# Attention, Mish layer and experts in one kernel: beside attention only eight first products, held unactivated; Mish and every second product behind it

## The chip, the cores and the metric

One core of one Trainium2 chip runs the whole program in one launch. The metric is device time in microseconds: 1038.68 us, median of 3 runs (1038.64 to 1038.86).

## The reference

Three stages follow each other; inputs are float32, the weights of the second stage float64.

```
a      = near(q,k,v) + repeat4(far(mean4(q), mean4(k), mean4(v)))   # 2 batches, 8 heads, 576 positions, 64 wide
         # near: softmax over keys less than 4 away; far: softmax over all 144 means of 4
x      = a as [1152 tokens, 512]
h      = x @ w_in            # 512 -> 2048
x      = (h * tanh(log1p(exp(h)))) @ w_out         # Mish, 2048 -> 512
P      = exp(x @ w_gate), then 8 rounds of row and column normalization
out    = sum over 8 experts e of P[:, e] * (relu(x @ w1[e]) @ w2[e])
```

## The kernel before

**Stages.** (1) Attention, for 12 tiles of 96 tokens. A tile has a near part: scores on TensorE (PE), row maxima on VectorE (DVE), exponentials on ScalarE (ACT, `pl`), scaling on DVE, transposes on PE, their copy on ACT (`pt`), values on PE, then `join` on DVE, `xhi` on ACT and `xlo` on DVE (lines 852 to 872). The far part (`pg`) is alike, per half batch. `xhi` and `xlo` are the layer's input split in two, so that a float32 product is three matmuls: hi x hi, hi x lo, lo x hi. (2) The Mish layer. Its 2048 inner columns are 8 blocks `j` of 256, a block is two chunks of 128, and the tokens are three groups `g` of 384 (four tiles). A chunk has a first product (12 matmuls of 384 columns: `x @ w_in`), Mish, and a second product (12 matmuls onto four banks of PSUM). `SEGS` (line 31) lists in which order groups and blocks go; a chunk's second product stands `LAG` = 4 chunks behind its first. (3) The experts.

**Who sets the order.** Attention is ordered by a planner (`Plan`, line 146): every step has an engine and a cost in `COST` (line 38); `lay` lays the steps out many times with varied priorities, and the best of `PASSES` tries is emitted, each engine's order fixed by `pin` (line 579). Where PE would wait, it inserts small filler matmuls (`warm`, line 594). Beside attention the plan also takes 12 chunks (groups 0 and 1, blocks 0 to 2): 12 first products (`p_gemm1`, line 946), their Mish as nine steps, all from the exponentials' table (Exp, clamp, product, Ln, product, Exp, product, `ghi`, `glo`, lines 973 to 993), and 8 second products (`p_gemm2`, line 995). It also converts the first six weight pieces from float64 (`p_raw`, `p_split`) and four halves more.

Behind it stands the loop (line 1090, 28 steps): `w_raw` and `w_split` convert weights, then `gemm1(s)` and `gemm2(s - LAG)`. Here Mish is one ACT function (`mish`, line 504), from another table. The loop is ordered by the Tile scheduler; `tc.issue_after(last["pe"])` (line 1101) holds the instructions of its block on PE, and on PE only, behind the plan's last PE instruction. ACT's table loads are put in by the compiler wherever the next function needs another table.

The last eight chunks and the experts are laid out by a second planner run (`plan2`). It takes the PSUM banks from a ring (`RB2`, line 1120); its first matmuls are L1219 (`p_half1`).

Of the kernel before, what the change touches and what calls it, by code (L numbers as in the profile page):

```python
# [8 lines left out]
F32 = mybir.dt.float32  # L9
# [8 lines left out]
TQ = 96  # L18
# [12 lines left out]
SEGS = [(0, (0, 1, 2)), (1, (0, 1, 2)), (2, (0, 1, 2, 3, 4, 5)), (1, (3, 4, 5)), (0, (3, 4, 5)), (0, (6, 7)), (1, (6, 7)),  # L31
# [10 lines left out]
    "qk": ("ACT", 0.375, 0.5), "means": ("DVE", 0.67, 0.75), "small": ("DVE", 0.08, 0.14), "max": ("DVE", 0.5, 0.58), "fmax": ("DVE", 0.37, 0.45),  # L42
# [3 lines left out]
    "vsum": ("DVE", 0.34, 0.42), "vsum2": ("DVE", 0.6, 0.68), "e": ("ACT", 0.38, 0.53), "clamp": ("POOL", 0.64, 0.68), "m": ("DVE", 0.48, 0.56),  # L46
    "ln": ("ACT", 0.51, 0.62), "mh": ("DVE", 0.47, 0.55), "inv": ("ACT", 0.415, 0.53), "g": ("DVE", 0.475, 0.56),
    "ghi": ("ACT", 0.415, 0.55), "glo": ("POOL", 1.08, 1.13), "raw": ("ACT", 0.56, 0.68), "shift": ("DVE", 0.34, 0.45),
    "sign": ("DVE", 0.62, 0.71), "tail": ("DVE", 0.62, 0.71), "whi": ("ACT", 0.53, 0.68), "wlo": ("POOL", 1.25, 1.3),
    "sum": ("ACT", 0.375, 0.53), "load": ("SP", 0.45, 0.0),  # L50
# [22 lines left out]
PORT = {"shift", "sign", "tail", "m", "g", "scale", "fscale", "guard", "vsum", "vsum2", "clamp", "glo", "wlo", "wsum", "form", "formlo", "wl", "formlo2", "mult", "pairlo", "sums", "lows"}  # L73
# [14 lines left out]
EXTRA = 4  # L88
# [10 lines left out]
SEED, SEED2, NOISE, OTHER, SLACK = 11, 21, 0.1, 0.3, 5.0  # L99
# [228 lines left out]
def attn_moe_moe_kernel(  # L328
# [44 lines left out]
    def f32(a):  # L373
        return a.bitcast(F32)
# [9 lines left out]
    two = ap.tile([128, 48], F32, name="two", bufs=1)  # L384
# [14 lines left out]
    DVE.memset(two, 2.0)  # L399
# [18 lines left out]
    loads = []  # L418
    for i, (g, j, _, _) in enumerate(items):
        if i == 0 or j not in [x[1] for x in loads[-NBUF:]]:  # L420
            loads.append((i, j))
    last_of = {g: max(i for i, x in enumerate(items) if x[0] == g) for g in range(len(TPG))}
    ATT_END = 2 * next(i for i, x in enumerate(items) if x[0] == len(TPG) - 1)

    order = [j for _, j in loads]
    need = {(kind, m): 2 * loads[m][0] + LAG * (kind == 2) for m in range(len(order)) for kind in (1, 2)}
# [47 lines left out]
    def w_split():  # L474

        n = place["split"]
        place["split"] += 1
        kind, m = ring[n]
        hi, lo = (new(ap, [128, 1024], F32R, f"{z}{kind}", NBUF) for z in ("hi", "lo"))
        split(wraw.pop(n), hi, lo)  # L480
        whl[kind, order[m]] = hi, lo

    def ends():

        out = []
        for m, (i, j) in enumerate(loads):
            again = [x for x, y in loads[m + 1:] if y == j]
            out.append(max(x for x, y in enumerate(items) if y[1] == j and x < (again or [len(items)])[0]))
        return out

    def free_at(n):

        kind, m = ring[n]
        if m < NBUF:
            return 0
        return 2 * sorted(ends()[:m])[m - NBUF] + 2 + (LAG if kind == 2 else 0)
# [6 lines left out]
    gq, acc, ysum, gl = {}, {}, {}, {}  # L503
    def mish(hps, n):

        ghi, glo = (new(ap, [128, NMAX], F32R, z, LAG)[:, 0:n] for z in ("ghi", "glo"))
        ACT.activation(out=hps, in_=hps, func=AF.Mish)
        last["mish"] = ACT.activation(out=ghi, in_=hps, func=AF.Copy)
        DVE.tensor_tensor(out=glo, in0=hps, in1=f32(ghi), op=ALU.subtract)
        return ghi, glo  # L510

    def gemm1(s):
# [10 lines left out]
        gq[s] = mish(bk, n)  # L523
# [84 lines left out]
    def fixed(ts):  # L608
# [10 lines left out]
    mt = ap.tile([128, 6 * NMAX], F32, name="mt", bufs=1)  # L619
    RE, RMM, RL = (Ring(2, lambda i, o=o: mt[:, NMAX * (2 * o + i):NMAX * (2 * o + i + 1)]) for o in range(3))  # L620
    RGH, RGL = (tiles(ap, [128, NMAX], F32R, z, LAG) for z in ("ghi", "glo"))
    ys0, ys1 = new(yp, [128, 3 * NMAX], F32, "ysum", 1), new(ap, [128, NMAX], F32, "ysum1", 1)
    RYS = Ring(1, lambda i: [ys0[:, NMAX * d:NMAX * d + NMAX] for d in range(3)] + [ys1])

    RRAW = Ring(RAWB, raw_place)
    RHL = {kind: Ring(NBUF, lambda k, kind=kind: tuple(new(ap, [128, 1024], F32R, f"{z}{kind}", NBUF)
                                                       for z in ("hi", "lo"))) for kind in (1, 2)}
# [181 lines left out]
    def p_near(t):  # L809
# [60 lines left out]
        add("xhi", lambda: ACT.activation(out=hi_, in_=y(), func=AF.Copy), r=[("b", id(bk))], w=[("xhi", t)], b=[bk])  # L870
# [4 lines left out]
    late = 2 * NBUF  # L875
# [50 lines left out]
    def p_split(n):  # L926
        kind, m = ring[n]
        y = rawb[n]
        wbuf[kind, order[m]] = z = Buf(RHL[kind])

        def whi(c):
            whl[kind, order[m]] = z.t
            ACT.activation(out=z.t[0][:, c], in_=y.t[:, c], func=AF.Copy)
# [9 lines left out]
    gbuf, accb, ysb = {}, {}, {}  # L943
    piece = {(kind, order[m]): n for n, (kind, m) in enumerate(ring[:late])}

    def p_gemm1(s):
# [29 lines left out]
        def glo_():
            POOL.tensor_tensor(out=v_(go), in0=v_(e), in1=f32(v_(gh)), op=ALU.subtract)
            gq[s] = v_(gh), v_(go)

        add("e", lambda: ACT.activation(out=v_(e), in_=hps(), func=AF.Exp), r=[("h", s)], w=[("e", s)], b=[bk, e], rank=1)  # L980
        add("clamp", lambda: POOL.tensor_scalar(out=v_(e), in0=v_(e), scalar1=EXP20, scalar2=0.0, op0=ALU.min, op1=ALU.max),
            w=[("e", s)], b=[e], rank=1)
        add("m", lambda: DVE.scalar_tensor_tensor(out=v_(m), in0=v_(e), scalar=2.0, in1=v_(e), op0=ALU.add, op1=ALU.mult),
            r=[("e", s)], w=[("m", s)], b=[e, m], rank=1)
        add("ln", lambda: ACT.activation(out=v_(l), in_=v_(m), func=AF.Ln, bias=two[:, 0:1], scale=1.0), r=[("m", s)],
            w=[("l", s)], b=[m, l], rank=1)
        add("mh", lambda: DVE.tensor_tensor(out=v_(e), in0=v_(m), in1=hps(), op=ALU.mult), r=[("m", s), ("h", s)],
            w=[("e", s)], b=[bk, m, e], rank=1)
        add("inv", lambda: ACT.activation(out=v_(l), in_=v_(l), func=AF.Exp, scale=-1.0), w=[("l", s)], b=[l], rank=1)
        add("g", lambda: DVE.tensor_tensor(out=v_(e), in0=v_(e), in1=v_(l), op=ALU.mult), r=[("l", s)], w=[("e", s)],  # L990
            b=[e, l], rank=1)
        add("ghi", ghi_, r=[("e", s)], w=[("ghi", s)], b=[e, gh], rank=1)
        add("glo", glo_, r=[("e", s), ("ghi", s)], w=[("glo", s)], b=[e, gh, go], rank=1)

    def p_gemm2(s):
        g, j, h, first, end = chunks[s]
        n = groups[g][1] * TQ
        z, (gh, go) = wbuf[2, j], gbuf[s]
        if end:
            ysb[g] = Buf(RYS)  # L1000
        for d in range(KD):
            if first:
                accb[g, d] = Buf(RB, "acc")
                accb[g, d].kept = g == len(TPG) - 2
            bk = accb[g, d]
            o = slice(128 * d, 128 * d + 128)

            def pe(d=d, bk=bk, o=o):
                whi, wlo = (x.rearrange("p (a b) -> p a b", a=2) for x in z.t)
                acc[d] = bk.t  # L1010
                ghi, glo = gq[s]
                for i, (a, b) in enumerate(((whi, ghi), (whi, glo), (wlo, ghi))):
                    PE.matmul(out=bk.t[:, 0:n], lhsT=a[:, h, o], rhs=b, start=(first and i == 0), stop=(end and i == 2))
                if d == KD - 1:
                    gq.pop(s)
            add("gemm2", pe, r=[("ghi", s), ("glo", s)] + [(x, piece[2, j], i) for x in ("whi", "wlo") for i in range(2)],
                w=[("acc", g, d), "gemm2"], b=[bk, z, gh, go], rank=1)
            if end:

                def keep(d=d, bk=bk):  # L1020
                    ysum[g] = ysb[g].t
                    ACT.activation(out=ysum[g][d][:, 0:n], in_=bk.t[:, 0:n], func=AF.Copy)
                add("sum", keep, r=[("acc", g, d)], w=[("ys", g, d)], b=[bk, ysb[g]], rank=1)
# [56 lines left out]
    mine = [banks.index(accb[len(TPG) - 2, d].t) for d in range(KD)]  # L1080
# [9 lines left out]
    for s in range(ATT_END, S0):  # L1090
# [606 lines left out]
```

## Time and profile before

| | |
|---|---|
| median of 3 runs | 1038.68 us |
| profiled execution | 1039.66 us, of it 1037.7 us span |
| busy share of the span | PE 99%, DVE 68%, ACT 52%, POOL 40% |
| attention with its products | up to 136 us |
| loop of the Mish layer | 136 to 254 us |
| last chunks and experts | 254 to 1037.7 us |

The profile is of one execution. Busy is the time in which an engine had an instruction under way; matmuls overlap, so PE's cost is better read from the distance between starts.

### The profile page before, as it was taken

The page shows a single profiled execution, that of the slowest core. Times are in us where ns is not written, and L with a number is a line of the kernel's source. Part 1 is how long each engine was busy: PE and PEld are TensorE (multiplying, and loading weights), DVE is VectorE, ACT ScalarE, POOL GpSimd, SP SyncE. Part 2 cuts the span into 40 slices and gives each one's busy share as a digit, 9 for nine tenths or more (in the row PEclk, how much of TensorE's full clock was granted, in tenths as well). Part 3 has the DMA queues.
Part 4 walks back from the last instruction along what each step waited for, and adds up shares of the span by engine and source line. Part 5 has one row for each costly group of instructions (what it writes and reads, how often), then busy time and mean ns, then how long its engine had stood idle before and what let it go on. Part 6 is the DMA issues. An engine that isn't in the chain of part 4 may idle for free.

```text
span 1037.7 us, 17431 instructions
## 1 busy us (share of the span) xinstructions
PE 1027.7 (99%) x6421; PEld 933.0 (90%) x6421; DVE 709.4 (68%) x1359; ACT 535.5 (52%) x1378; POOL 413.8 (40%) x459
## 2 busy tenths in 40 slices
PE   8999999999999999999999999999999999999998
PEld 5888899999999988998999899989998899889997
DVE  6998854444578988876675766586666577657844
ACT  6888884434458434543545355534553455345531
POOL 0135232112236529553544254424552445345530
PEclk9999999999999999999999999999999999999999
DMA  9673212221004101210212012102120121111002
GB/s 217 169 169 92 78 61 83 85 78 42 1 11 132 54 8 62 62 56 5 62 61 62 1 62 62 62 1 61 62 62 7 55 61 62 25 37 61 22 1 92
DMA packets 47997, 63.41 MB, mean 61 GB/s; under 512 B 15272, under 2 KB 31656, under 8 KB 47912
## 3 DMA queue, kind: packets, MB, share of 16 engines
q1 hardware_dynamic: 47912, 62.30, 20.8%
q8 instruction: 50, 0.82, 0.3%
q14 instruction: 35, 0.29, 0.1%
HBM read 59.93 MB, written 2.36 MB: 60 GB/s over the span
## 4 chain that ended last, share of the span: by engine, by line
PE 73%; DVE 2%; ACT 1%; DMA 0%; issue 0%; DVEq 0%; ACTq 0%
PE bank L1612 38%; PE bank L1560 30%; PE bank L1237 2%; PE bank L1219 2%; PE bank L1392 1%; DMA raws<-in_moe_w_dram 0%; PE bank L1401 0%; DVE ysum L547 0%; DVE bank L1302 0%; ACT hhi L1377 0%; PE bank L1489 0%; DVE raws L464 0%; DVE hlo L1380 0%; ACT xs L1575 0%; ACT L1464 0%
## 5 line engine op out<-in xcount | busy, mean ns | idle before, releaser
L1575 ACT ACTIVATE xs<-bank 128x384 f32<-128x384 f32 x231 | 113.4, 492 | 262.2 <-PE bank L1560 240.8
L1612 PE MATMUL bank<-xs,hhi 128*128 128x512 f32 (+1 forms) x760 | 235.7, 391 | 0.0
L1628 DVE SCALAR_TENSOR_TENSOR yacc<-bank,P,yacc 128x512 f32<-128x512 f32 (+1 forms) x217 | 161.0, 747 | 93.6 <-PE bank L1612 92.0
L1612 PEld LDWEIGHTS bank<-xs,hhi 128*128 128x128 f32 x760 | 140.6, 188 | 19.7
L1535 POOL TENSOR_TENSOR wops<-wsums,wops 128x256 fp32r<-128x256 f32 x114 | 86.2, 767 | 160.9 <-ACT wops L1533 160.8
L1612 PE MATMUL bank<-xs,hlo 128*128 128x512 f32 (+1 forms) x380 | 148.8, 392 | 0.0
L1302 DVE TENSOR_TENSOR bank<-bank,xs 128x384 f32<-128x384 f32 x189 | 98.9, 560 | 46.4 <-ACT xs L1575 37.1
L1612 PE MATMUL bank<-wc,hhi 128*128 128x512 f32 x398 | 122.9, 390 | 0.0
L1560 PE MATMUL bank<-xform,wops 128*128 128x384 f32 x558 | 106.2, 335 | 0.0
L1560 PEld LDWEIGHTS bank<-xform,wops 128*128 128x128 f32 x558 | 98.0, 188 | 4.4
L1380 DVE SCALAR_TENSOR_TENSOR hlo<-bank,hhi 128x384 fp32r<-128x384 f32 x150 | 78.8, 550 | 16.3 <-ACT hhi L1377 13.8
L1612 PEld LDWEIGHTS bank<-wc,hhi 128*128 128x128 f32 x398 | 74.5, 188 | 15.5
L1377 ACT ACTIVATE hhi<-bank 128x384 fp32r<-128x384 f32 x150 | 70.4, 487 | 34.7 <-DVE bank L1302 29.8
L1302 DVE TENSOR_TENSOR wsums<-raws 128x256 f32<-128x256 f32 x147 | 63.5, 446 | 35.9 <-POOL wops L1535 17.9
L1612 PEld LDWEIGHTS bank<-xs,hlo 128*128 128x128 f32 x380 | 71.3, 188 | 16.2
L1612 PE MATMUL bank<-wc,hlo 128*128 128x512 f32 x199 | 78.2, 393 | 0.0
L1535 POOL TENSOR_TENSOR ysum<-wsums,ysum 128x256 fp32r<-128x256 f32 x59 | 45.0, 769 | 75.9 <-ACT ysum L1533 75.9
L1560 PE MATMUL bank<-xhi,wops 128*128 128x384 f32 x252 | 70.8, 337 | 0.3 <-ACT xs L1575 0.3
L1533 ACT ACTIVATE wops<-wsums 128x256 fp32r<-128x256 f32 x114 | 45.5, 413 | 33.6 <-PE bank L1560 28.6
L1422 POOL TENSOR_TENSOR xs<-temp,xs 128x512 fp32r<-128x512 f32 x42 | 58.4, 1412 | 9.9 <-ACT xs L1420 9.9
L472 POOL TENSOR_TENSOR lo<-raws,hi 128x512 fp32r<-128x512 f32 x20 | 26.5, 1338 | 75.2 <-ACT hi L471 69.4
L1560 PE MATMUL bank<-xform,ysum 128*128 128x384 f32 x282 | 54.8, 335 | 0.0
(241 smaller groups left out, 2255.5 us busy)
## 6 DMA issues: line engine op xcount, KB each, us to landing
temp<-in_moe_w_dram SPq DMA_DIRECT2D x64, 256.0 KB
raws<-in_moe_w_dram SPq DMA_DIRECT2D x16, 768.0 KB
raw<-in_moe_w_in_dram SPq DMA_DIRECT2D x16, 512.0 KB
raw<-in_moe_w_out_dram SPq DMA_DIRECT2D x16, 512.0 KB
raws<-in_moe_w_dram SPq DMA_DIRECT2D x5, 512.0 KB
rawq<-in_q_dram SPq DMA_DIRECT2D x4, 576.0 KB
rawv<-in_v_dram SPq DMA_DIRECT2D x8, 288.0 KB
vw<-in_v_dram SPq DMA_DIRECT2D x12, 192.0 KB
```

The costliest lines, as they stand in the source:

```text
L472: POOL.tensor_tensor(out=lo[:, c], in0=raw[:, c], in1=f32(hi[:, c]), op=ALU.subtract)
L1219: PE.matmul(out=bk.t[:, 0:NMAX], lhsT=a[:, kk, o], rhs=b[:, kk, c0:c0 + NMAX], start=(i == 0), stop=(i == 11))
L1302: eng.tensor_tensor(out=out, in0=a, in1=b, op=ALU.add if cb > 0 else ALU.subtract)
L1377: ACT.activation(out=hb.t[0], in_=bk.t[:, 0:TH], func=AF.Relu)
L1380: DVE.scalar_tensor_tensor(out=hb.t[1], in0=bk.t[:, 0:TH], scalar=0.0, in1=f32(hb.t[0]), op0=ALU.max, op1=ALU.subtract)
L1422: add("wlo", lambda raw=raw, y=y: POOL.tensor_tensor(out=y.t[:, 1], in0=raw(), in1=f32(y.t[:, 0]), op=ALU.subtract), r=[("r2", c), ("ch", ...
L1533: add("wh", lambda src=src, y=y: ACT.activation(out=y.t[:, 0], in_=piece(src), func=AF.Copy), r=key + rk, w=[("wh", r, n)] + wk, b=[y] + bs)
L1535: add("wl", lambda src=src, y=y: POOL.tensor_tensor(out=y.t[:, 1], in0=piece(src), in1=f32(y.t[:, 0]), op=ALU.subtract), r=key + [("wh", r ...
L1560: PE.matmul(out=bb.t[:, 0:TH], lhsT=y.t[:, wz, kk, :], rhs=x[xz][:, kk, :], start=(fresh and i == 0), stop=(i == 3 * KH - 1), skip_group_c ...
L1575: add("keep", lambda src=src, y=y: ACT.activation(out=y.t, in_=src.t[:, 0:TH], func=AF.Copy), r=[key, "late"], w=[("b", id(y))], b=[src, y])
L1612: PE.matmul(out=bk.t[:, a:b], lhsT=h[hz][:, js], rhs=y[:, wz, a:b], start=(f == fs[0] and i == 0), stop=(f == fs[-1] and i == 2))
L1628: DVE.scalar_tensor_tensor(out=y, in0=bk.t[:, a:b], scalar=p, in1=y, op0=ALU.mult, op1=ALU.add)
```

## The change

- `SEGS` starts with group 2 and goes on with 1 and 0 (before: 0, 1, 2). Only the four pairs (group, block) in `HELD`, eight chunks of groups 0 and 1, get their first product beside attention. Its result is copied to SBUF as it is, by ACT and DVE in turn (`holdA`, `holdD`), into the eight `ghi` and `glo` buffers that the loop uses later.
- The nine Mish steps, all second products and the partial sums (`ysum`) leave the plan. Attention may take six banks of PSUM at a time (before four).
- The plan converts three weight pieces and four halves (`LATE` = 3) instead of six and four.
- The loop has all 40 steps: for a held chunk only Mish, for the others first product and Mish; `gemm2(s - LAG)` from the fourth step on. Until the held chunks are through, `ghi` and `glo` lie in `xform`.
- `plan2` takes its banks in the order in which the loop has left them. Some buffers move, and the planner's seed is another.

```diff
+HELD = [(0, 0), (0, 1), (1, 0), (1, 1)]
-SEGS = [(0, (0, 1, 2)), (1, (0, 1, 2)), (2, (0, 1, 2, 3, 4, 5)), (1, (3, 4, 5)), (0, (3, 4, 5)), (0, (6, 7)), (1, (6, 7)),
+SEGS = [(2, (0, 1, 2)), (1, (0, 1, 2)), (0, (0, 1, 2, 3, 4, 5)), (1, (3, 4, 5)), (2, (3, 4, 5)), (0, (6, 7)), (1, (6, 7)),
...
-MOST = {"start": 8, "waves": 4, "gemm1": 1, "acc": 4}
+MOST = {"start": 8, "waves": 6, "gemm1": 2}
...
-    def mish(hps, n):
-
-        ghi, glo = (new(ap, [128, NMAX], F32R, z, LAG)[:, 0:n] for z in ("ghi", "glo"))
+    def mish(s, hps):
+
+        if s < SWITCH:
+            ghi, glo = (xform[:, s % (LAG + 1), z].rearrange("p a b -> p (a b)")[:, 0:NMAX] for z in range(2))
+        else:
+            ghi, glo = (new(ap, [128, NMAX], F32R, z, LAG) for z in ("ghi", "glo"))
         ACT.activation(out=hps, in_=hps, func=AF.Mish)
...
+    held_ = [new(ap, [128, NMAX], F32R, z, LAG) for z in ("ghi", "glo") for _ in range(LAG)]
...
-        add("e", lambda: ACT.activation(out=v_(e), in_=hps(), func=AF.Exp), r=[("h", s)], w=[("e", s)], b=[bk, e], rank=1)
...
+        def hold(i):
+            y = held[s] = f32(held_[i])
+            if i % 2:
+                DVE.tensor_copy(out=y, in_=bk.t[:, 0:n])
+            else:
+                ACT.activation(out=y, in_=bk.t[:, 0:n], func=AF.Copy)
+        i = len(held)
+        held[s] = None
+        add("holdD" if i % 2 else "holdA", partial(hold, i), r=[("h", s)], w=[("held", s)], b=[bk], rank=1)
...
-    for s in range(ATT_END):
+    for s in sorted((s for s, x in enumerate(chunks) if x[:2] in HELD), key=lambda s: chunks[s]):
         p_gemm1(s)
-        if s >= LAG:
-            p_gemm2(s - LAG)
...
-    for s in range(ATT_END, S0):
+    SWITCH = max(held) + 1
+    for s in range(S0):
...
         with tc.issue_after(last["pe"]):
-            gemm1(s)
-            gemm2(s - LAG)
+            if s in held:
+                mish(s, held.pop(s))
+            else:
+                gemm1(s)
+            if s >= LAG:
+                gemm2(s - LAG)
...
-    RB2 = Ring(8, lambda i: banks[i], MOST2)
+    w_, turn_ = of_tag["w"], turn["w"]
+    spots = w_[turn_ % 4 + 1:] + w_[:turn_ % 4] + [acc[d] for d in range(KD)] + [w_[turn_ % 4]]
+    RB2 = Ring(8, lambda i: spots[i], MOST2)
```

ACT's order in attention, in before, behind the last copies of kT (`pl`: near exponentials, `mt` and `ghi`: steps of Mish, `raws` and `hi`: weight conversion):

```order
L980 ACTIVATE mt<-bank_119 128x384
L905 ACTIVATE raws<-raw_1012 128x512
L974 ACTIVATE ghi<-mt 128x384
L870 ACTIVATE xhi<-bank_115 128x4x96
L985 ACTIVATE mt<-mt,two 128x384
L738 ACTIVATE pl_103,ld<-bank_120,lm 96x102
L989 ACTIVATE mt<-mt 128x384
L738 ACTIVATE pl_103,ld<-bank_120,lm 96x102
L905 ACTIVATE raws<-raw_1078 128x512
L738 ACTIVATE pl_103,ld<-bank_120,lm 96x102 x2
L980 ACTIVATE mt<-bank_116 128x384
L738 ACTIVATE pl_102,ld<-bank_117,lm 96x102 x3
```

and at the like place of the changed program, from the first hold on (L955; L495 is the Mish of the loop, here on a held chunk in `ghi`; L721 are the exponentials; L891 a weight half):

```order
L955 ACTIVATE ghi<-bank_118 128x384
L891 ACTIVATE raws<-raw_991 128x512
L495 ACT_TABLE_LOAD
L495 ACTIVATE ghi<-ghi 128x384
L721 ACT_TABLE_LOAD
L721 ACTIVATE pl_101,ld<-bank_115,lm 96x102 x4
L721 ACTIVATE pg_103,gd<-bank_111,gm 72x144 x2
L721 ACTIVATE pg_104,gd<-bank_117,gm 72x144 x2
L495 ACT_TABLE_LOAD
L495 ACTIVATE ghi<-ghi 128x384
L721 ACT_TABLE_LOAD
L721 ACTIVATE pg_106,gd<-bank_118,gm 72x144
```

The steps of Mish between the exponentials are gone; in their place stand Mish instructions of the loop, each between two table loads. The whole order has eight Mish of held chunks in front of attention's last `xhi` (L855) and, from this place to there, eleven table loads.

PE's order where the plan ends and the loop begins, in before (L957 planned first products, L540 second and L521 first products of the loop):

```order
L957 MATMUL bank_118<-xlo,hi_1088 128x384
L957 MATMUL bank_118<-xhi,lo_1089 128x384
L540 MATMUL bank_116<-ghi,hi_1352 128x384
L521 MATMUL bank_114<-xhi,hi_484 128x384
L540 MATMUL bank_116<-glo,hi_1352 128x384
L540 MATMUL bank_116<-ghi,lo_1353 128x384
```

and in the changed program (L838 the value products of the last attention tile, L942 planned first products, L509 first products of the loop):

```order
L942 MATMUL bank_117<-xhi,lo_646 128x384
L838 MATMUL bank_112<-pt,vw_96 64x96 x8
L509 MATMUL bank_113<-xhi,hi_471 128x384
L509 MATMUL bank_115<-xhi,hi_471 128x384
L509 MATMUL bank_116<-xhi,hi_645 128x384
L509 MATMUL bank_113<-xlo,hi_471 128x384
```

Before, the plan ends with first products of chunks whose tiles are long done; now it ends with a tile's values, and the loop's first products read that tile.

## Rows read from the trace of the kernel before

**Rows 1.** the page: busy time and share of the span; granted clock by slice

```profile
PE 1027.7 (99%) x6421; PEld 933.0 (90%) x6421; DVE 709.4 (68%) x1359; ACT 535.5 (52%) x1378; POOL 413.8 (40%) x459
...
PEclk9999999999999999999999999999999999999999
```

**Rows 2.** busy time in two stretches: us, then PE, PEld, DVE, ACT, POOL

```profile
14.00:136.00 122.00, 119.21 (x1599) 101.42 (x1596) 109.57 (x251) 105.92 (x404) 34.09 (x33) 1.00 0.54 132
300.00:1037.70 737.70, 734.05 (x3689) 660.49 (x3687) 517.31 (x978) 344.75 (x819) 335.04 (x385) 1.00 0.15 48
```

**Rows 3.** PE in order of time, the seam: start us, us, instruction

```profile
136.03 0.34 PE L540 MATMUL bank<-ghi,hi 128*128 128x384 f32 x1
```

**Rows 4.** line 540 on PE: durations ns, first to last start us

```profile
L540 PE MATMUL bank<-ghi,lo x112: 336/336/338, 136.5 to 252.3; 128*128 128x384 f32 x112
```

**Rows 5.** PE in order of time, behind the loop: idle before and its releaser

```profile
253.90 0.45 PE L1219 MATMUL bank<-xhi,hi 128*128 128x384 f32 x1 [1.23 <-DVE glo L509]
```

**Rows 6.** groups of instructions, 0 to 136 us: count, busy us, mean ns, idle

```profile
L985 ACT ACTIVATE mt<-mt,two 128x384 f32<-128x384 f32 x11 | 6.8, 619 | 2.0 <-DVE mt L983 2.0
L977 POOL TENSOR_TENSOR glo<-mt,ghi 128x384 fp32r<-128x384 f32 x10 | 11.2, 1117 | 20.0 <-issue 15.6 <-ACT ghi L974 4.4
```

**Rows 7.** PE in order of time, where both orders are cut

```profile
65.10 0.45 PE L957 MATMUL bank<-xhi,hi 128*128 128x384 f32 x1
```

**Rows 8.** PE in order of time, small matmuls between products

```profile
120.10 0.34 PE L957 MATMUL bank<-xlo,hi 128*128 128x384 f32 x1
120.36 0.67 PE L780 MATMUL bank<-ident,pg 72*72 72x72 f32 x8
...
121.14 0.42 PE L957 MATMUL bank<-xhi,lo 128*128 128x384 f32 x1
121.40 0.34 PE L957 MATMUL bank<-xhi,hi 128*128 128x384 f32 x1
```

**Rows 9.** groups of instructions, 0 to 136 us: the narrow fillers

```profile
L598 PE MATMUL bank<-identb 128*128 128x96 bf16 x47 | 3.0, 207 | 0.0
```

**Rows 10.** ACT in order of time, attention: a cost is the distance of starts

```profile
71.91 0.68 ACT L905 ACTIVATE raws<-raw 128x512 f32<-128x512 f32 x1
72.48 0.35 ACT L738 ACTIVATE pl<-bank,lm 96x102 f32<-96x102 f32 x1
...
72.80 0.35 ACT L738 ACTIVATE pl<-bank,lm 96x102 f32<-96x102 f32 x1
...
73.12 0.49 ACT L980 ACTIVATE mt<-bank 128x384 f32<-128x384 f32 x1
73.49 0.35 ACT L738 ACTIVATE pl<-bank,lm 96x102 f32<-96x102 f32 x1
...
74.45 0.65 ACT L933 ACTIVATE hi<-raws 128x512 fp32r<-128x512 f32 x1
74.97 0.36 ACT L738 ACTIVATE pl<-bank,lm 96x102 f32<-96x102 f32 x1
...
89.81 0.41 ACT L783 ACTIVATE pt<-bank 72x288 f32<-72x288 f32 x1
90.10 0.87 ACT L847 ACTIVATE pt<-bank 102x384 f32<-102x384 f32 x2
```

**Rows 11.** ACT in order of time, the seam: table loads and Mish

```profile
142.02 1.28 ACT L989 ACT_TABLE_LOAD   x1
143.32 0.52 ACT L989 ACTIVATE mt<-mt 128x384 f32<-128x384 f32 x1
...
147.54 0.47 ACT L507 ACTIVATE bank<-bank 128x384 f32<-128x384 f32 x1
148.05 0.49 ACT L508 ACTIVATE ghi<-bank 128x384 fp32r<-128x384 f32 x1
```

**Rows 12.** DVE in order of time: a tile's join and its xlo

```profile
130.18 0.57 DVE L861 TENSOR_TENSOR bank<-bank,odT 128x384 f32<-128x384 f32 x1 [0.28 <-PE bank L855]
...
131.58 0.55 DVE L871 TENSOR_TENSOR xlo<-bank,xhi 128x384 fp32r<-128x384 f32 x1
```

More of the change, by code (lines that the diff above doesn't have):

```diff
@@ L416, in attn_moe_moe_kernel @@
     NS = len(chunks)
[L418 to L421, printed above, removed]
     last_of = {g: max(i for i, x in enumerate(items) if x[0] == g) for g in range(len(TPG))}
-    ATT_END = 2 * next(i for i, x in enumerate(items) if x[0] == len(TPG) - 1)
-    order = [j for _, j in loads]
-    need = {(kind, m): 2 * loads[m][0] + LAG * (kind == 2) for m in range(len(order)) for kind in (1, 2)}
+    uses = {1: [(j, i) for i, (g, j, _, _) in enumerate(items) if (g, j) not in HELD], 2: [(x[1], i) for i, x in enumerate(items)]}
+    firsts = {(kind, j): min(i for x, i in u if x == j) for kind, u in uses.items() for j in range(NQ)}
+    lasts = {(kind, j): max(i for x, i in u if x == j) for kind, u in uses.items() for j in range(NQ)}
+    need = {z: 2 * i + (LAG if z[0] == 2 else 0) for z, i in firsts.items()}
     ring = sorted(need, key=need.get)
@@ L477, in w_split @@
         place["split"] += 1
-        kind, m = ring[n]
+        kind, j = ring[n]
         hi, lo = (new(ap, [128, 1024], F32R, f"{z}{kind}", NBUF) for z in ("hi", "lo"))
         split(wraw.pop(n), hi, lo)
[L481 to L489, printed above, removed]
+        whl[kind, j] = hi, lo
     def free_at(n):
-        kind, m = ring[n]
-        if m < NBUF:
+        kind, j = ring[n]
+        before = [x for k, x in ring[:n] if k == kind]
+        if len(before) < NBUF:
             return 0
-        return 2 * sorted(ends()[:m])[m - NBUF] + 2 + (LAG if kind == 2 else 0)
+        return 2 * lasts[kind, before[-NBUF]] + 2 + (LAG if kind == 2 else 0)
     for tag, n, dt in (("raw64", R64, U32), ("hi1", NBUF, F32R), ("lo1", NBUF, F32R), ("hi2", NBUF, F32R), ("lo2", NBUF, F32R)):
@@ L509, in mish @@
         DVE.tensor_tensor(out=glo, in0=hps, in1=f32(ghi), op=ALU.subtract)
-        return ghi, glo
+        gq[s] = ghi, glo
     def gemm1(s):
@@ L869, in p_near, with xhi_ @@
         add("join", join, r=[("od", b, half, i) for i in range(2)], w=[("b", id(bk))], b=[bk, od])
-        add("xhi", lambda: ACT.activation(out=hi_, in_=y(), func=AF.Copy), r=[("b", id(bk))], w=[("xhi", t)], b=[bk])
+        def xhi_():
+            last["mish"] = ACT.activation(out=hi_, in_=y(), func=AF.Copy)
+        add("xhi", xhi_, r=[("b", id(bk))], w=[("xhi", t)], b=[bk])
         add("xlo", lambda: DVE.tensor_tensor(out=lo_, in0=y(), in1=f32(hi_), op=ALU.subtract),
@@ L874, in attn_moe_moe_kernel @@
     r64, rawb = {}, {}
-    late = 2 * NBUF
+    late = LATE
     def p_load64(m):
@@ L941, in p_split @@
             add("wlo", partial(wlo, c), r=[("raw", 2 * n + i), ("whi", n, i)], w=[("wlo", n, i)], b=[y, z])
-    gbuf, accb, ysb = {}, {}, {}
-    piece = {(kind, order[m]): n for n, (kind, m) in enumerate(ring[:late])}
+    piece = {x: n for n, x in enumerate(ring[:late])}
     def p_gemm1(s):
@@ L987, in p_gemm1 @@
[L987 to L1023, printed above, removed]
@@ L1074, in attn_moe_moe_kernel @@
         p_half(i + 1)
[L1075 removed]
+    for s in sorted((s for s, x in enumerate(chunks) if x[:2] in HELD), key=lambda s: chunks[s]):
         p_gemm1(s)
[L1077 to L1078 removed]
     plan.run(PASSES, SEED, True)
[L1080 to L1081 removed]
+    over = [max((u.done for u in o.users), default=0.0) if o else 0.0 for o in RB.own]
+    free = sorted(range(8), key=lambda i: over[i])
+    of_tag.update(w=[banks[free[(i - 1) % 4]] for i in range(4)], acc=[banks[i] for i in free[4:]])
     place.update(load=2 * late + EXTRA + 2, raw=2 * late + EXTRA, split=late)
```

58 lines of the change are left out of this document (16 added, 42 removed), and 1 row of the table COST.

## The prediction

> **What bounds the kernel now.** I read the page first: TensorE is busy 99% of the span, at a granted clock of 0.9 or more in every slice, which is the 2.4 GHz level [rows 1]. A busy share of 99% says little about any one stage, so the stretches come next. In the attention stretch (14 to 136 us) three engines are nearly full together: PE 119.2, DVE 109.6 and ACT 105.9 of 122 us. Behind 300 us, the third stage, PE has 734.1 of 737.7 us and DVE and ACT about 70% and 47% [rows 2]. So the third stage is PE's alone, and attention is where an edit of ACT or DVE can count. Last I read PE in order of time at the seams. The last planned product starts one step before 136.03, where the loop's first matmul (L540) starts without a gap [rows 3]; the loop's last starts at 252.3 [rows 4]. The 28 pairs of products are 672 matmuls, so one costs (252.3 - 136.03) / 671 = 0.1733 us: the loop has no wait in it. At its end stands one, 1.23 us before L1219 at 253.90, for the `glo` of the last chunk [rows 5].
>
> So the sum has three terms: when the loop starts, how many matmuls it has, and the wait behind it. The third stage is left equal: on PE it has the same 2264 rows in the same 329 alternations of kind in both orders, though a few stand elsewhere around the gate.
>
> **What the loop gains.** Twelve chunks of first product and eight of second stood beside attention; now eight first ones do. Four first and eight second ones, 12 x 12 = 144 matmuls, move into the loop, which then has 816: 816 x 0.1733 = 141.4 us. ACT and DVE have room there: the eight held chunks need no first product, but by the order most of their Mish is already done, and the weights that move (three pieces) are converted one half per step as before. The wait behind the loop goes: before, the first bank taken is the one that the last chunk's Mish still reads; after, it is the one used three chunks earlier. I take the 1.23 us as gained, zero at worst.
>
> For break-even the loop must therefore start at 253.9 - 141.4 = 112.5 us, 23.5 us earlier than now.
>
> **What attention loses.** Each of the 12 chunks loses nine steps: on ACT four of 0.37 to 0.62 us, on DVE three of about 0.57, on POOL two, the dearer 1.12 [rows 6, 10, 12]. That frees 18 to 30 us of ACT and about 20 of DVE. Three pieces of weight less are six halves of 0.57 + 0.52 us on ACT [rows 10]. Four holds on ACT and four on DVE come in at 0.37 and about 0.57. All this lies beside PE and is worth only what PE waits for.
>
> To see what is left for PE I cut both orders at the same work. At 65.10 us in before PE has done 216 turn, 48 value and 64 near-score matmuls and 12 of first product (its next, L957, starts there) [rows 7]; in the changed order PE stands at exactly these counts behind its 12th matmul of first product, and with one filler less. Up to there nothing that PE waits for is removed (loads from HBM in the same order, the same conversions), so I take 65.1 us for both. Behind it, before takes 136.03 - 65.10 = 70.9 us: 228 matmuls of both products, 39.5 us; 31 blocks of them between small matmuls, each with two changes that make a start 0.26 us after the last instead of 0.17 [rows 8], 31 x 0.18 = 5.6; fillers 3.0 [rows 9]; so attention itself has 22.8. After keeps 22.8, has 84 matmuls, 14.6, in 18 blocks, 3.2, and two fillers: 40.6 us. By PE alone attention would end at 105.7.
>
> **What it adds, and the order shows this and not the diff.** A held chunk's Mish depends on nothing but its copy in SBUF, and the wrapper that keeps the loop's work behind the plan binds only PE. So all eight held Mish stand on ACT in front of the last `xhi` of attention, six of them in the middle of the softmax exponentials, which need another table. In front of that last `xhi` stand 11 ACT_TABLE_LOADs behind the cut, where before had none; before's four at the seam cost the loop nothing. One took 1.28 us, and the next activation started 1.30 us after it (142.02 to 143.32); a Mish of 128x384 took 0.51 to the next start [rows 11].
>
> The Trainium skill (ScalarE: Activation LUTs, "What ACT_TABLE_LOAD costs") gives the load the same 1283 ns, but adds about 1380 ns of drain to every switch. This trace shows the load and no such drain: the activation behind it starts 0.02 us after its end [rows 11]. By the page the 11 switches would cost 29.3 us, by the row 14.3.
>
> ACT's queue from the cut to the last `xhi`, counted in the changed order, at starts apart in [rows 10, 11]: 11 loads x 1.30 = 14.3; 8 Mish x 0.51 = 4.1; 48 exponentials x 0.32 = 15.4 (the 16 wider-row far ones priced as the near); 24 copies of 384 columns (transposed probabilities, `xhi`, qT, holds) x 0.37 = 8.9; 8 far ones x 0.29 = 2.3; 4 of odT at no more than that, 1.2; 4 halves of `hi` x 0.52 = 2.1; 2 raw halves x 0.57 = 1.1. Sum 49.4 us. Without loads, Mish and the four halves it is 28.9, which would have fitted under PE's 40.6 with 11.7 to spare. So ACT is late next: loads and Mish fill its spare time and 8.8 us more.
>
> Behind the cut comes the first hold and a raw half, so the 49.4 start at about 65.1 + 0.3 + 0.37 + 0.57 = 66.3 and end at 115.7. I walked ACT's rows against what PE and DVE must return: after most loads the operands are already there, since the engine comes late; a return trip of DVE, ACT, DVE takes 130.18 to 131.58 + 0.55, 1.95 us [rows 12], and the last load with its Mish covers the one behind the last exponentials. I put 1.0 us on the rest: 116.7. Then PE has nothing left: the plan now ends with the values of the last tile, directly followed by the first products of the third token group, which read that tile. Before had 30 matmuls to run there. Their first matmul needs `xhi`, the others `xlo`, 0.55 us later, partly covered by the first matmuls of two other chunks: 0.4. The loop so starts, in effect, at 117.1.
>
> **Sum.** 117.1 + 141.4 = 258.5 instead of 253.9: 4.6 us later. The profiled execution took 1039.66 us for a span of 1037.7, 0.98 over the median of the runs; the 4.6 is a difference inside the span, and I add it to the median: 1038.68 + 4.6 = 1043.3. Bounds: waits of ACT from 0 to 4, the hand-over 0 or 1.23, cut 65.1 give or take 1: 1041.5 to 1047.
>
> **Rivals.**
> - The loads run where ACT waits anyway, and PE stays the bound: end of attention 105.7, join, `xhi`, `xlo` 1.95, loop at 107.7, its end at 249.1: 4.8 us faster, 1033.9. For it: the scheduler put each Mish where it thought ACT idle, and a load issues without waiting for its operand. Against: the spare time is 11.7 us and the queue exceeds it by 8.8. It decides only if ACT enters the stretch 9 us ahead, which the first hold, waiting for PE, forbids.
> - About half of it: the softmax rows run early against PE's order, so that the loads cost 4 to 5 us less. The loop starts near 112.5, 1038 to 1040, no change. For it: three ring buffers more for attention in PSUM (six banks, not four).
> - The return trips are not overlapped: ACT's order was planned without the loads, and each of the six interruptions delays a tile by a whole trip, 6 x 1.95 = 11.7 instead of the 1.0: 1054. For it: ACT is in order, and [rows 2] shows DVE nearly as full as ACT. Against: DVE has lost about 20 us of work. A granted clock that falls when PE waits 2 to 3 us at a time, which no row here shows (the longest wait in them is the 1.23 of [rows 5]), would end in the same place.
> - Each switch costs more than its load: the engine runs empty before it and fills again behind it, at most two of the longest activations, 2 x 0.68 = 1.36 us a switch [rows 10]; 11 x 1.36 = 15.0, so 1058.3. For it: amid the exponentials the pipe is fuller than at the seam. Against: [rows 11]. The drain of the Trainium skill's page named above would be of this size.
>
> **Chances.** Forecast 0.64, faster rival 0.10, half way 0.10, return trips 0.13, emptying 0.03. The first lies wholly beyond 0.2% of the median (2.1 us, about what a measurement of this kernel can tell from no change), the half-way case wholly within: slower 0.80, same 0.10, faster 0.10. Range 1038.5 to 1050: it leaves out the faster rival and the far ends of the slow ones. The forecast's own range is 1041.5 to 1047.
>
> **What would show it.** Right: about ten table loads of 1.28 us on ACT between 65 and 117 us, ACT busy over 95% there, PE waiting some 9 to 11 us in that stretch for `pl`, `pt` or `xhi` of ACT; the loop's first L509 at 115.5 to 119; no gap within the loop, 0.173 us a matmul; no wait for `glo` in front of L1161. Wrong: the loop starting by 112 with ACT's loads in its idle time; a loop that waits for weights or for held chunks (the step of L495 and L496); or a clock below 1.00 behind 65 us.

## The result and the profile after

The changed kernel takes 1049.13 us (median of 4 executions, 1048.35 to 1053.03), the kernel before beside it 1038.66 (4 executions, 1038.22 to 1038.86): a ratio of 1.0109, 95% interval 1.0084 to 1.0134. It is slower by 10.5 us where 4.6 were forecast. The sign, the place and the mechanism came as forecast, the size did not: 1049.13 lies above the forecast's own range of 1041.5 to 1047 and only inside the wider one, 1038.5 to 1050, that left room for slow rivals. Each of the three terms of ACT's queue was a microsecond or more too small, and the clock did something that the forecast had left to a rival.

The page of the changed kernel, to be held against [rows 1]: TensorE's busy time is 1.2 us less, but the span is 9.2 us longer, and one slice of the granted clock, the fourth (79 to 105 us), is no longer at 9.

```profile
PE 1026.5 (98%) x6376; PEld 933.8 (89%) x6376; DVE 694.5 (66%) x1338; ACT 536.0 (51%) x1365; POOL 391.9 (37%) x435
...
PEclk9998999999999999999999999999999999999999
...
PE 90%; ACT 7%; DMA 2%; DVE 1%; issue 0%; DVEq 0%; ACTq 0%
```

The last line is from the chain that ended last: 7% of the span, some 70 us, run through ACT. So I looked at the two halves of attention behind the cut of [rows 7] (columns: stretch, length, then busy us of PE, PEld, DVE, ACT and POOL, granted clock, DMA share, GB/s).

```profile
65.00:95.00 30.00, 22.06 (x258) 17.65 (x260) 17.08 (x50) 28.89 (x86) 1.08 (x1) 0.90 0.16 35
95.00:125.00 30.00, 26.20 (x268) 22.92 (x265) 21.95 (x46) 25.43 (x82) 5.59 (x5) 0.99 0.28 82
```

In the first half ACT is busy 28.9 of 30 us while PE has 22.1: PE, full in [rows 2], now waits for ACT. The waits of PE between 65 and 136 us, by releaser (us in total, times, longest; before had two, 0.6 and 0.4):

```profile
PE bank L942 <- ACT pl L721: 2.4, 2, 1.9
PE bank L509 <- ACT xhi L855: 1.8, 1, 1.8
PE bank L803 <- ACT odT L788: 1.7, 1, 1.7
PE bank L828 <- ACT odT L788: 1.5, 1, 1.5
PE bank L838 <- ACT pt L830: 1.4, 1, 1.4
PE bank L763 <- ACT qT L667: 1.1, 1, 1.1
```

Together they and the smaller ones are 11.9 us, of which 11.3 end on ACT. ACT in order of time (start us, us, instruction, idle before and its releaser; the accumulator reads left out), first at the cut, then at the end of attention:

```profile
65.09 0.55 ACT L855 ACTIVATE xhi<-bank 128x384 fp32r<-128x384 f32 x1
65.46 0.56 ACT L955 ACTIVATE ghi<-bank 128x384 f32<-128x384 f32 x1
66.74 0.68 ACT L891 ACTIVATE raws<-raw 128x512 f32<-128x512 f32 x1 [0.72 <-DMA raw<-in_moe_w_out_dram]
67.44 1.28 ACT L495 ACT_TABLE_LOAD   x1
68.73 0.53 ACT L495 ACTIVATE ghi<-ghi 128x384 f32<-128x384 f32 x1
69.26 1.28 ACT L721 ACT_TABLE_LOAD   x1
70.56 0.34 ACT L721 ACTIVATE pl<-bank,lm 96x102 f32<-96x102 f32 x1
...
71.85 0.37 ACT L721 ACTIVATE pg<-bank,gm 72x144 f32<-72x144 f32 x1
72.21 0.38 ACT L721 ACTIVATE pg<-bank,gm 72x144 f32<-72x144 f32 x1
...
72.92 0.38 ACT L721 ACTIVATE pg<-bank,gm 72x144 f32<-72x144 f32 x1
73.41 1.28 ACT L495 ACT_TABLE_LOAD   x1
...
117.41 0.54 ACT L855 ACTIVATE xhi<-bank 128x384 fp32r<-128x384 f32 x1
119.17 0.63 ACT L463 ACTIVATE hi<-raws 128x512 fp32r<-128x512 f32 x1 [1.22 <-DVE raws L904]
119.71 0.51 ACT L495 ACTIVATE glo<-glo 128x384 f32<-128x384 f32 x1
120.12 0.48 ACT L855 ACTIVATE xhi<-bank 128x384 fp32r<-128x384 f32 x1
```

One held Mish (L495) amid the exponentials (L721) takes 67.44 to 70.56, 3.1 us, of which 2.6 are the two loads. Eleven loads stand between the cut and the last `xhi` (L855). On PE the 12th matmul of planned first products, behind which the prediction cut the order, starts at 63.73; the loop's first product follows the last `xhi`, and the third stage follows the loop's last product without the wait of [rows 5]:

```profile
63.73 0.33 PE L942 MATMUL bank<-xhi,lo 128*128 128x384 f32 x1
...
120.66 0.80 PE L509 MATMUL bank<-xhi,hi 128*128 128x384 f32 x3 [1.77 <-ACT xhi L855]
...
262.50 0.34 PE L528 MATMUL bank<-ghi,lo 128*128 128x384 f32 x1
262.67 0.34 PE L1161 MATMUL bank<-xhi,hi 128*128 128x384 f32 x1
```

### The profile page after: what moved, and what is told of

The parts are those of the page before. It is cut to its first block, busy times and chain, and to the rows that moved or that the text cites. A ratio compares the mean times of both kernels' runs of the same rounds, so it can differ in the third digit from the quotient of the medians.

```text
span 1046.9 us, 17277 instructions
## 1 busy us (share of the span) xinstructions
PE 1026.5 (98%) x6376; PEld 933.8 (89%) x6376; DVE 694.5 (66%) x1338; ACT 536.0 (51%) x1365; POOL 391.9 (37%) x435
## 4 chain that ended last, share of the span: by engine, by line
PE 90%; ACT 7%; DMA 2%; DVE 1%; issue 0%; DVEq 0%; ACTq 0%
PE bank L1554 38%; PE bank L1502 30%; PE bank L528 7%; PE bank L509 6%; PE bank L1179 2%; ACT pl L721 2%; PE bank L1161 2%; DMA raw<-in_moe_w_out_dram 1%; ACT pg L721 1%; ACT L495 1%; ACT L721 1%; PE bank L1334 1%; DMA rawq<-in_k_dram 0%; PE bank L654 0%; PE bank L1343 0%; PE bank L781 0%
## 5 line engine op out<-in xcount | busy, mean ns | idle before, releaser
L1554 PE MATMUL bank<-xs,hhi 128*128 128x512 f32 x760 | 235.7, 391 | 0.0
L1554 PE MATMUL bank<-xs,hlo 128*128 128x512 f32 x380 | 148.9, 392 | 0.0
L464 POOL TENSOR_TENSOR lo<-raws,hi 128x512 fp32r<-128x512 f32 x26 | 34.3, 1327 | 167.8 <-ACT hi L463 154.9
```

What stands on the lines that cost most here:

```text
L1554: PE.matmul(out=bk.t[:, a:b], lhsT=h[hz][:, js], rhs=y[:, wz, a:b], start=(f == fs[0] and i == 0), stop=(f == fs[-1] and i == 2))
```

## The experiments

The theory was that ACT's queue behind the cut, lengthened by loads and Mish, sets the start of the loop. Its rivals: the new order of attention is slow by itself; the return trips; the clock. In the changed kernel and its nine variants what lies behind the loop's first product (span less its start) is 926.2 to 927.8 us in the profiled execution, so that start is the number to read. Where two kernels have the same attention and differ only in a filled wait in front of the loop (the last three experiments), their starts lie 0.4 to 1.0 us apart: 107.36 and 106.33, 105.88 and 105.47, 120.66 and 121.22. No difference of that size is read as an effect. The kernel before, run beside each batch, had medians of 1038.65 to 1038.96. The start stands here with the loads and the Mish that ACT runs between the cut and the last `xhi`:

| kernel | loads | Mish | loop starts | median (executions) |
|---|---|---|---|---|
| changed | 11 | 8 | 120.66 | 1049.13 (1048.35 to 1053.03) |
| all held Mish behind | 0 | 0 | 105.88 | 1034.29 (1034.02 to 1035.77) |
| Exp for held Mish | 0 | 8 Exp | 107.36 | 1035.54 (1034.29 to 1037.05) |
| first four behind | 3 | 4 | 109.49 | 1038.35 (1036.77 to 1039.25) |
| last four behind | 8 | 4 | 117.64 | 1047.78 (1046.47 to 1048.51) |
| weight copies behind | 11 | 8 | 119.60 | 1048.65 (1047.99 to 1053.91) |

**All held Mish behind attention.** In the loop, and nothing else:

```
+    plan_end = last["mish"].ins          # the last xhi
 ...
             if s in held:
-                mish(s, held.pop(s))
+                with tc.issue_after(plan_end):
+                    mish(s, held.pop(s))
```

> The changed kernel, with one more order: the eight Mish steps of the held products (the Mish, its high part on ACT, the rest on DVE) may not be issued on ACT ahead of the last xhi of attention. Nothing else is changed. Theory (ACT's queue): in the changed kernel 11 table loads of 1.28 us and seven or eight Mish of 0.51 us, some 18 us, stand on ACT ahead of the last xhi at 120.1; without them ACT would be through at about 102, and TensorE's own work (40.6 us behind the first hold, so 105.7, with a microsecond or two of waits) sets the start of the loop at 107 to 109 instead of 120.7. The loop keeps its 142 us and the third stage its 784: 1035 to 1037. Rival (the new order of attention is slow by itself: no second products between attention's steps to fill TensorE, so it waits for transposes and copies as long as before): the loop starts at 117 or later, and the time stays above 1044. Rival (the Mish come due at the start of the loop and TensorE waits for them there): the loop is longer by 4 us or more, 1039 to 1042.

Measured: 1034.29 us, 0.9962 of before (0.9949 to 0.9974), so 14.8 less than the changed kernel and 4.5 less than before. ACT in this kernel, at the end of attention:

```profile
105.33 0.49 ACT L855 ACTIVATE xhi<-bank 128x384 fp32r<-128x384 f32 x1 [0.31 <-DVE bank L844]
105.72 0.67 ACT L453 ACTIVATE raws<-raw 128x512 f32<-128x512 f32 x1
106.41 1.28 ACT L495 ACT_TABLE_LOAD   x1
107.70 1.77 ACT L495 ACTIVATE glo<-glo 128x384 f32<-128x384 f32 x4
```

and PE there:

```profile
103.27 0.88 PE L838 MATMUL bank<-pt,vw 102*64 102x96 f32 x16
105.88 0.79 PE L509 MATMUL bank<-xhi,hi 128*128 128x384 f32 x3 [1.72 <-ACT xhi L855]
```

One load and the eight Mish now follow the last `xhi`. PE's own work in attention ends at 104.2, and the loop starts at 105.88, behind a wait of 1.72 us for that `xhi`. Both rivals fall: the new order of attention is faster than before's (the loop starts 6.6 us ahead of the break-even of 112.5), and the loop (to 247.86) takes 142.0 us, as in the changed kernel, without a wait for the late Mish.

**Exp in place of the held Mish.** The same instructions, no second table:

```
-        ACT.activation(out=hps, in_=hps, func=AF.Mish)
+        ACT.activation(out=hps, in_=hps, func=AF.Exp if s in exps else AF.Mish)   # exps: the held chunks
```

> The changed kernel, with Exp in place of Mish in the eight held chunks alone: the same instructions in the same order, but without a change of function table between attention's exponentials and the held chunks. It leaves Mish out of these chunks. Theory (table loads): ten or eleven loads of 1.28 us go, some 13 to 14 us of ACT's queue; the eight Exps of about 0.5 us stay. ACT is through at about 106 to 107, TensorE at 105.7 plus waits, so the loop starts at 107 to 110: 1036 to 1039. Rival (the return trips of the small products, not the loads, hold TensorE): 1045 to 1049. Rival (the loads cost only where TensorE is not waiting for something else, half of them): about 1042.

Measured: 1035.54 us, 0.9970 of before (0.9958 to 0.9981). The loop starts 13.3 us earlier than in the changed kernel, and 14.3 in the repeat of this attention with the filled wait (106.33). So of the 14.8 the loads are 13.3 to 14.3, 1.2 to 1.3 a load, and the Mish themselves the 0.5 to 1.5 that are left. This is what the loads were worth and not an upper bound of what one costs, because PE's own work, to 104.2, is the next limit. In its profile the clock fell behind the wait in front of the loop (columns as in the windows above):

```profile
104.00:107.00 3.00, 1.60 (x21) 1.16 (x19) 2.78 (x6) 1.78 (x5) 0.42 (x1) 1.00 0.06 16
107.00:110.00 3.00, 2.64 (x12) 2.50 (x13) 2.37 (x4) 1.05 (x3) 0.86 (x1) 0.82 0.50 164
110.00:113.00 3.00, 3.00 (x13) 3.00 (x12) 0.21 (x1) 2.70 (x4) 1.27 (x1) 0.62 0.62 173
```

PE is 1.60 busy of the 3 us before 107; behind that it runs 13 matmuls in 3 us instead of 19, and what follows the loop's start takes 927.8 us instead of 926.2.

**The bank order alone, in the kernel before.**

```
-    RB2 = Ring(8, lambda i: banks[i], MOST2)
+    RB2 = Ring(8, lambda i: spots[i], MOST2)     # spots as in the change
```

> The kernel before, with one part of the change alone: the order in which the third stage's plan is given the eight PSUM banks (the banks of the first products but one, then those of the second products). Theory: the one wait of TensorE at the start of the third stage (1.23 us, at 253.9, for the last subtraction of a low part) goes, as it went in the changed kernel, and nothing else moves: 1037.4, faster by 1.2. Rival: the wait turns into another one of the same length a few products later, or the plan's other waits grow: 1038.4 to 1039.5.

Measured: 1037.1 us (11 executions), 0.9987 of before (0.9978 to 0.9995), 0.5 to 2.3 us less (1.7 by the medians). The 1.23 us lie within that, and PE has no idle time left in front of the third stage's first product (L1221 in this kernel):

```profile
251.16 0.34 PE L540 MATMUL bank<-ghi,lo 128*128 128x384 f32 x1
251.33 0.34 PE L1221 MATMUL bank<-xhi,hi 128*128 128x384 f32 x1
```

The term "the wait behind the loop goes" holds by itself.

**The loop's own weight copies behind attention as well.** Beside the edit of the first experiment:

```
-            w_split()
+            with tc.issue_after(plan_end):
+                w_split()
```

> As the run with the held Mish behind attention, and the high parts of the weight pieces that the loop splits for itself (four ACT copies of 0.52 us that were issued among attention's steps, one of them in front of the last xhi, where it waited 1.2 us for DVE) also behind the last xhi. Theory: ACT is no longer what ends last once the Mish are gone, so that this gives at most the one wait back, 0 to 1.5 us: 1034 to 1036.5. Rival (the first weight pieces of the loop are then late, since each needs the copy and then a subtraction of 1.25 us on POOL): TensorE waits in the loop, and the time is 1037 to 1041.

Measured: 1034.81 us (1033.92 to 1035.69), 0.9962 (0.9949 to 0.9976), no different from the first. The loop starts at 104.87, 1.0 earlier, but its first second product (113.93) waits 0.37 us for a held Mish's high part, which the copies now delay, and the span is the same 1032.1. Of the other 0.6, half lies in the loop and half in the third stage; what costs it there is not shown.

**Four of the eight behind, the first or the last.** The next two kernels ask whether each microsecond of ACT counts:

```
+    late_ = sorted(held, key=lambda s: chunks[s])[:4]     # or [4:]
 ...
-            if s in held:
+            if s in late_:
+                with tc.issue_after(plan_end):
+                    mish(s, held.pop(s))
+            elif s in held:
                 mish(s, held.pop(s))
```

> The changed kernel with the first four of the eight held Mish steps (those issued on ACT between 67 and 84) put behind the last xhi; the last four stay among attention's steps. That takes 8 of the 11 table loads and 4 Mish out of ACT's queue, all of them more than 30 us ahead of the last xhi. Theory (ACT's queue is full from the first hold to the last xhi, so each of its microseconds counts wherever it stands): 8 x 1.29 + 4 x 0.51 = 12.4 us less: the loop starts at 108 to 109, 1036.5. Rival (what stands early is made up for later, only the last loads in front of the last tile delay the start): no more than half of it, 1043 or later.

> The counterpart: the last four held Mish steps (those issued on ACT between 102 and 120) behind the last xhi, the first four as in the changed kernel. The same number of Mish moves, but only 3 table loads go with them. Theory (queue): 3 x 1.29 + 4 x 0.51 = 5.9 us less, the loop starts at about 115: 1043. Rival (only what stands near the end counts): about as much as moving all eight, 1034 to 1038. Rival (the number of Mish, not of loads, decides): the same as with the first four moved.

Measured: the first four are worth 11.2 us of the loop's start (1038.35 us, 0.9995 of before, 0.9986 to 1.0004), near the 12.4 expected, though they stood over 30 us ahead of the last `xhi`. Part of the missing 1.2 is TensorE's clock: behind a wait of 1.43 us for ACT it lay at its lower level for a time, and attention's last transposes took 1.52 us instead of 0.87 (columns as above).

```profile
105.00:108.00 3.00, 3.00 (x24) 2.75 (x24) 2.52 (x5) 1.59 (x4) 0.00 (x0) 0.67 0.02 5
```

The last four are worth 3.0 (1047.78 us, 1.0087, 1.0073 to 1.01) where 5.9 were expected. Four Mish each: the count of Mish does not decide. By the loads it is 8 against 3. But the queue theory in its plain form falls for the last third of attention. There, in the kernel with the last four behind, ACT, free of a pair of loads, waited almost as long for DVE (ACT's line first, then DVE, then POOL):

```profile
104.46 0.34 ACT L721 ACTIVATE pl<-bank,lm 96x102 f32<-96x102 f32 x1 [2.60 <-DVE lm L713]
```

```profile
101.72 1.49 DVE L895 TENSOR_SCALAR raws<-raws 128x512 uint32<-128x512 uint32 x1
103.25 0.69 DVE L900 SCALAR_TENSOR_TENSOR raws<-raw,raws 128x512 uint32<-128x512 uint32 x1
103.86 1.55 DVE L713 TENSOR_REDUCE lm<-bank 96x4 f32<-96x408 f32 x3
```

```profile
101.25 1.68 POOL L464 TENSOR_TENSOR lo<-raws,hi 128x512 fp32r<-128x512 f32 x1 [6.44 <-ACT hi L463]
```

The maxima (L713) that the next exponentials need stand on DVE behind a weight half's shift (L895), which took 1.49 us beside a subtraction on POOL; the median of the ten shifts is 0.416. The two kernels with the weight copies behind test this: the POOL subtraction is not beside it, and the same shift takes 0.41 and 0.42 us; in the eight others it takes 1.49 to 1.51. In the one with the copies alone behind:

```profile
101.77 0.41 DVE L895 TENSOR_SCALAR raws<-raws 128x512 uint32<-128x512 uint32 x1
```

It is only part of the wait: with Mish and copies behind, ACT still waits 1.7 us for the maxima there, with the Mish alone behind 2.3. In the changed kernel the pair of loads at 102 lay over that wait and cost 0.5 us instead of 3.1.

**The weight copies alone behind.** The edit of `w_split` above, without that of the held Mish.

> The changed kernel with its Mish steps where they were, and only the four ACT copies of 0.52 us for the loop's own weight pieces put behind the last xhi. Theory (queue): 4 x 0.52, and the 1.2 us for which the last of them waited for DVE in front of the last xhi, go: 3.3 us less, 1045.6. With the Mish behind as well the same edit gave nothing, since ACT was no longer what ended last; here it is. Rival (these copies stood in time that ACT had over): the wait alone or nothing, 1047.7 to 1049.

Measured: 1048.65 us (1.0105 of before, 1.0087 to 1.0123); the loop starts 1.06 us earlier, not 3.3. The rival is right. ACT in this kernel, at the end:

```profile
116.34 0.55 ACT L855 ACTIVATE xhi<-bank 128x384 fp32r<-128x384 f32 x1
118.59 0.52 ACT L495 ACTIVATE glo<-glo 128x384 f32<-128x384 f32 x1 [1.69 <-DVE glo L953]
119.06 0.49 ACT L855 ACTIVATE xhi<-bank 128x384 fp32r<-128x384 f32 x1
```

With the copy gone, the last Mish in front of the last `xhi` waits as long, for the last hold on DVE (L953). At the end of attention ACT ran at DVE's pace, with the copy in front or without it.

**Filling PE's wait in front of the loop.** The Exp kernel, and seven matmuls on constants behind attention's last product:

```
     plan.run(PASSES, SEED, True)
 ...
+    warm(35, free[3], False)      # seven of 128x480, to a bank nobody reads
```

> The kernel with Exp in the held chunks (it leaves Mish out of them), and seven matmuls of 128x480 on constants (about 0.2 us each, results unused) on TensorE between the last product of attention and the loop, where TensorE waited 1.4 us for the last xhi. In the profile of the run without them the granted clock was 0.82 and 0.62 in the two stretches of 3 us right behind that wait, and the loop took 143.3 us instead of 141.9. Theory (the wait of TensorE is what lowers the clock): the clock stays at 1.00 there and the loop takes 141.9; the median comes down from 1035.5 to 1034.2 and the executions lie closer together than 1034.3 to 1037.1. Rival (the clock falls for another reason, or falls in some executions anyway): no change, 1035.5. Rival (the seven run longer than the wait and delay the loop): 1036 or more.

Measured: 1034.68 us (1034.27 to 1035.17), 0.9962 of before (0.9948 to 0.9976); the clock stays at 1.00, the loop starts at 106.33 and what follows takes 926.3 us, 1.5 less than behind the fall.

```profile
107.00:110.00 3.00, 3.00 (x19) 3.00 (x18) 1.69 (x3) 1.19 (x2) 0.50 (x1) 1.00 0.23 76
110.00:113.00 3.00, 3.00 (x19) 3.00 (x19) 0.88 (x2) 2.93 (x6) 0.80 (x1) 1.00 0.55 169
```

The wait does not lower the clock each time: the profiled execution of the first experiment has the same wait, 1.72 us, and 1.00 behind it.

**The same in the first experiment's kernel.**

> The run with the eight held Mish behind attention, and the seven matmuls on constants between the last product of attention and the loop, under the 1.7 us for which TensorE waits there. Theory (the wait lowers the clock in some executions, and costs the loop 1.4 us in those): of the five executions without the seven, two had a granted clock of 0.998 and 1035.7 us, three 0.999 to 1.000 and 1034.0 to 1034.3; with them all lie at 1034.0 to 1034.5, clock 1.0. Rival (clock falls elsewhere): two kinds of executions as before. Rival (the seven delay the loop): 1034.5 or more in all.

Measured: 1034.34 us (1033.62 to 1034.63), 0.9954 of before (0.9940 to 0.9967). Two of five executions had lain at 1035.7, now none of five does; the two medians are the same within their spread. The two pairs together carry the argument: without the seven, five of eleven executions had a clock of 0.998 and took 1035.7 us or more; with them none of ten did. So filling the wait is what keeps the clock up there. It does not account for every slow execution: one with the weight copies behind took 1035.69 at 1.000. This is the version to keep: the new order of attention, the Mish behind it, PE's wait filled.

**The same in the changed kernel.**

> The changed kernel, its Mish where they were, with the seven matmuls on constants in front of the loop, where TensorE waited 1.77 us. Its executions lay at 1048.35 to 1053.03 with clocks of 0.997 to 0.991. Theory A (what varies is the clock at the start of the loop, behind this wait): the executions come together at 1047.5 to 1049. Theory B (the clock falls in attention's stretch of 84 to 97, behind two waits for ACT, as the profile shows, and that varies): the seven change nothing, the median stays at 1048.5 to 1049.5 and single executions may still lie at 1053.

Measured: 1049.44 us (1048.17 to 1052.56), 1.0104 of before (1.009 to 1.0117): nothing changed, theory B. The clock falls here in mid-attention: in this profile it is 0.50 from 72.5 to 75.5 us and from 90 to 96.

## Why the prediction was right, and where its size was off

- **The start of ACT's queue: 66.3 forecast, 67.3 measured.** The raw half in front of the loads waited 0.72 us for its DMA; the step "Behind the cut comes the first hold and a raw half" took the load for landed. The cut itself was also misplaced: PE was through with its 12th matmul of first products at 63.9, not 65.1. That gained nothing, since ACT was the later engine already: the `xhi` at 65.09 stands in front of the hold, which did not wait for PE, as "the first hold, waiting for PE" has it.
- **Its length: 49.4 forecast, 50.8 measured.** From 67.31 to the end of the last `xhi` at about 120.5 are 53.2 us, 2.3 of them waits. 0.6 of the excess are the 16 far exponentials, 0.36 us apart (71.85 to 72.21) and not 0.32. Most of the rest is that a load does not overlap with what stands in front of it: from the exponential at 72.92 to the load at 73.41 are 0.49 us instead of 0.36, and at eight of the eleven loads the distance is longer in this way, by 0.12 to 0.18. The 11 loads were right in number and price: the exponential at 70.56 follows a load that ends at 70.54. The Trainium skill (ScalarE: Activation LUTs, "What ACT_TABLE_LOAD costs") would have each switch drain for some 1380 ns more. This row does not show it, nor does the queue, which is 1.4 us longer than with eleven loads at 1.30 and would have been some 15 longer.
- **Its waits: 1.0 forecast, 2.3 measured**, 1.2 of them in front of the last `xhi`, for DVE. Here the step "I walked ACT's rows against what PE and DVE must return" failed: it followed the tiles' return trips, not the weight halves that DVE converts in between. Two experiments show how far this goes: around 102 us DVE holds ACT for 2.6 of the 3.1 us that the pair of loads took, and at the end for 1.7 us, as long as the last weight copy and its wait had taken.
- **The loop: 141.4 forecast, 142.0 measured; no wait in it, none behind it.** As forecast, at 0.174 us a matmul. The third stage took 784.2 us against 783.8.
- **Sum.** The last `xhi` ends 3.8 us later than forecast; the first product follows it 0.2 sooner than allowed for: 3.6; loop 0.6, third stage 0.4. That makes 9.2 in the span for 4.6. The other 1.2 of the medians' 10.5 come from the two profiled executions: that of before took 0.98 us more than its median, that of after 0.26 less.
- **Its own signs.** Eleven loads, ACT 96% busy from 65 to 117 us, 11.9 us of waits of PE and no gap in the loop or behind it are as announced, or nearly. The loop's first product at 120.66 is outside the announced 115.5 to 119, and a clock below 1.00 behind 65 us, listed as a sign of being wrong, did occur.
- **The rivals.** "The loads run where ACT waits anyway" (1033.9) looks like what happens once nothing stands in ACT's queue (1034.29), but the match is in part luck. PE's work in attention was priced well, 40.6 us forecast and 40.2 measured (63.9 to 104.2), while the cut lay 1.2 earlier and the hand-over was shorter, so that the loop starts at 105.88 and not at 107.7; the loop, the third stage and the 1.2 of the profiled executions made up for it. "Return trips not overlapped" is what the last third shows on a small scale. "Each switch costs more than its load" (1058.3) is refuted by the length of the queue; the Exp kernel alone could not refute it, since PE limits what it can gain. "A granted clock that falls when PE waits" came true, in part: between the two waits that end at 88.84 and 90.80 PE was busy 0.62 of 3 us, and then the clock lay at its lower level (columns as in the windows above).

```profile
87.00:90.00 3.00, 0.62 (x2) 0.00 (x0) 2.43 (x7) 2.97 (x4) 0.00 (x0) 0.82 0.00 0
90.00:93.00 3.00, 2.20 (x20) 1.96 (x20) 0.00 (x0) 2.99 (x13) 0.00 (x0) 0.50 0.50 183
93.00:96.00 3.00, 3.00 (x37) 2.67 (x36) 1.64 (x3) 2.41 (x10) 1.27 (x1) 0.54 0.04 8
```

  In that stretch it cost little, since ACT is the later engine: up to 97 us ACT's only waits there are 0.17, 0.39 and 0.56 us, so at most 1.1 in this execution. The kernel with the last four behind had a second such fall, at 72 to 78 us, where the one with the weight copies behind had none; ACT's first exponential behind its wait came at 93.63 in the one and at 93.73 in the other.

Open stays this: in each of the three kernels with all 11 loads among attention one of four or five executions took 1052.6 to 1053.9 us, at a granted clock of 0.990 or 0.991 over the span. None of these was the profiled one, so where they lose 4 us isn't shown; the wait in front of the loop isn't it, since filling it changed nothing. A low clock alone does not cost as much: the profiled execution with the last four behind had 0.991, from three falls (at 71, 88 and 119 us), and took 1047.34 us, 0.4 less than its kernel's median.

## What to carry to other kernels

Ask of a scheduler's freedom, not only of the code's place: a step written behind a stage moves into it on every engine that nothing binds, and two functions of different tables that alternate on ACT cost a load each way. Where the engine is full, hold such steps back by an explicit order and let them share one load; here that one order turned a loss of 10.5 us into a gain of 4.5, of which the new order of the banks alone gives 1.7 by the medians. A queue sum is a lower bound for each engine by itself: before pricing the last microseconds of one, look at what the next later engine would make it wait for.

## What was not expected of the hardware

- The clock falls after some waits of PE and not after others. A wait of 2.41 us at 71.6 in one kernel was followed by 0.50 to 0.51 for 6 us; one of 2.43 at 71.7 in another, with the same rows around it, by 1.00. The Trainium skill (TensorE: Matmul & The Clock Gate, "HAM oscillation — how this bites in real kernels") describes waits between matmuls after which the clock falls. The runs agree that it can: with the wait in front of the loop unfilled the mean clock was 0.998 in five of eleven executions, filled in none of ten.
- A DVE shift of 128x512 took 1.49 us beside a POOL subtraction of 1.68 us and 0.416 otherwise (median of ten); it ended 0.28 us behind the POOL instruction. In the two kernels without that subtraction beside it the same shift took 0.41 and 0.42.
